# Moving a skip term from diagonal matmuls to GpSimd, with tanh gates and early parameters, in a scan-and-gate kernel

## The chip, the cores and the metric

The kernel runs on one core of one Trainium2 chip. The metric is the device time of one execution in microseconds (us); most numbers are medians of several runs. The kernel before takes 203.13 us (median of 3 runs, 202.52 to 203.82).

Engines are named as in the profile: PE is TensorE (PEld its weight loads), DVE is VectorE, ACT is ScalarE, POOL is GpSimd, SP is the engine that issues most DMA. A name with q after it (ACTq) is that engine's sequencer.

## The reference

The input has 2048 tokens of width D = 448; types are bf16. After a layer norm two branches read the same `xn`: a state-space scan over time, and a gated feed-forward block of width F = 1792.

```python
def _A_ref(x, ...):                     # scan branch, complex state of 448
    Bu = einsum("bld,pd->blp", x, B_bar)
    for t in range(L):
        h = Lam_bar * h + Bu[:, t, :]
    return 2.0 * einsum("blp,dp->bld", hseq, Cmat).real + x * Dskip   # the skip term

def _B_ref(x, w_gate, w_up, w_down):    # feed-forward branch
    h = sigmoid(x @ w_gate) * (x @ w_up)
    return h @ w_down

x = A_x
xn = layernorm(x)
s = _A_ref(xn, ...)
g = silu(_B_ref(xn, w_gate, w_up, w_down))
return x + s * g
```

## The kernel before

The 2048 tokens go through in four chunks of 512, each of four tiles of 128. Every operation is handed to a small planner with an engine, an estimated cost and its dependences; the planner then fixes the order on each engine. So a change of one part can reorder all. TensorE makes, for each chunk, 14 gate and up groups ("gu" buffers in PSUM, three of them), the scan's input groups (also in "gu"), four down groups and four output groups y (two "acc" buffers). VectorE does the scan and its rotations.

The parts that the change touches:

```python
# gate and up evacuation, chunks 1 to 3: ScalarE empties both halves of PSUM
add("ACT", ..., lambda: A.activation(sig[b][:], gu[a][:], ACT.Sigmoid), ...)
...
add("ACT", ..., lambda: A.copy(out=ub[b][:], in_=gu[a][:]), r=[("gu", a)], w=[("ub", b)])
add("DVE", ..., lambda: V.tensor_tensor(out=ho, in0=sig[sb_][:], in1=ub[b][:], op=ALU.mult), ...)

# chunk 0 already uses tanh, and VectorE reads the up half from PSUM:
#   ho = (tanh(gate / 2) + 1) * up

# down output: silu as sigmoid times copy
add("ACT", ..., lambda: A.activation(sigd[b][:], d, ACT.Sigmoid, scale=half), ...)
add("ACT", ..., lambda: A.activation(zb[b][:], d, ACT.Copy, scale=half), ...)
add("DVE", ..., lambda: V.tensor_tensor(out=g_t[g][:], in0=zb[b][:], in1=sigd[b][:], op=ALU.mult), ...)

# output group y: the skip term xn * Dskip as four matmuls with a diagonal matrix
for i, (hm, cm) in enumerate(K_ORDER):
    T.matmul(y, lhsT=hT[c % 2][:, hm, js], rhs=cT[:, cm, c0:c1], start=(i == 0), stop=(i == 6))
    if i:
        continue
    for k in range(4):
        ...
        T.matmul(y[:, a0 - c0:a1 - c0], lhsT=xnT[c % 3][:, 2 * k, js], rhs=diag[:, a0:a1], ...)
...
add("DVE", ..., lambda: V.tensor_tensor(out=od, in0=y, in1=g_t[g][:, c0:c1], op=ALU.mult), ...)
add("DVE", ..., lambda: V.tensor_tensor(out=od, in0=od, in1=x_all[:, t, c0:c1], op=ALU.add), ...)
```

The scan's parameters (three vectors, and Dskip) are loaded last on GpSimd's queue, and the cos/sin tables are made from them in the middle of chunk 0.

## Time and profile before

| | before |
|---|---|
| time, median of 3 | 203.13 us |
| span of the profiled run | 199.6 us |
| TensorE, VectorE, ScalarE, GpSimd busy | 184.7, 157.7, 115.5, 42.8 us |
| TensorE clock | 1.00 in all windows but the last (the clock records begin at 13.72 us) |

From the page of the kernel before: the busy time of each engine, with its share of the span and number of instructions, then rows of busy tenths in 40 equal slices of the span, of 5.0 us here.

```profile
PE 184.7 (93%) x1479; PEld 91.9 (46%) x1486; DVE 157.7 (79%) x298; ACT 115.5 (58%) x160; POOL 42.8 (21%) x94
PE   7498999994999999997998999999999999999991
DVE  4700599998999999999999999997897999340163
POOL 6400387258261181062061000000000000000000
```

TensorE is the fullest engine. VectorE shows a row of nines, with one eight, from about 25 to 135 us. GpSimd has nothing at all to do after about 110 us.

The table of ten-microsecond windows of the kernel before. The columns are the window and its length, then busy us (and instructions) of PE, PEld, DVE, ACT and POOL, then the granted TensorE clock, the DMA share and GB/s.

```profile
10.00:20.00 10.00, 9.12 (x196) 7.68 (x194) 0.00 (x0) 5.72 (x6) 0.23 (x1) 1.00 1.17 244
...
40.00:50.00 10.00, 7.02 (x62) 3.04 (x58) 9.25 (x16) 9.88 (x17) 6.86 (x16) 1.00 0.96 243
...
100.00:110.00 10.00, 9.16 (x70) 4.61 (x71) 9.79 (x21) 6.87 (x9) 4.04 (x7) 1.00 0.23 60
...
150.00:160.00 10.00, 9.97 (x74) 5.07 (x75) 8.71 (x14) 7.06 (x11) 0.00 (x0) 1.00 0.01 2
```

Between 10 and 20 us VectorE does nothing. Between 40 and 50 us TensorE loses 3 us while ScalarE is full. In the 100 to 110 window VectorE is at 98% and TensorE at 92%. The 1.00 of the first window hides a slow start: the timeline shows TensorE's matmuls of the first gate groups 0.106 us apart until 13.73 us and 0.055 after that, and the clock records only begin at 13.72.

Groups of instructions of the kernel before (line, engine, operation, output and inputs, count, then busy us, mean ns of one, and idle time before them with its cause).

```profile
L727 DVE TENSOR_TENSOR_SCAN wv<-c_r,st,z 128x512 bf16<-128x512 f32 x18 | 22.9, 1279 | 0.2
L639 DVE TENSOR_TENSOR hF<-sig,ub 128x1024 bf16<-128x1024 bf16 x21 | 14.3, 686 | 4.0 <-ACT ub L638 3.9
L741 DVE TENSOR_TENSOR ta<-wv,cosT 128x1024 bf16<-128x1024 bf16 x12 | 8.1, 678 | 0.1
L822 PE MATMUL acc<-diag,xnT 128*128 128x128 bf16 (+1 forms) x60 | 5.4, 212 | 0.0
```

The timeline of VectorE in the same kernel (start, duration) shows what one instruction costs when others follow at once: they overlap a little, so the step from start to start is the better measure, 0.60 us for `ta`, 1.19 us for the scan.

```profile
95.23 0.69 DVE L741 TENSOR_TENSOR ta<-wv,cosT 128x1024 bf16<-128x1024 bf16 x1
...
97.67 1.28 DVE L727 TENSOR_TENSOR_SCAN wv<-c_r,st,z 128x512 bf16<-128x512 f32 x1
```

What TensorE waited for (total us, times, longest) was most of all ScalarE, emptying PSUM:

```profile
PE gu L660 <- ACT sig L628: 3.4, 2, 2.3
```

And the head on ScalarE in the kernel before (the first square root of the layer norm starts at 4.79 us):

```profile
3.05 1.28 ACT L328 ACT_TABLE_LOAD   x1 [3.05 <-issue]
...
4.79 0.30 ACT L356 ACTIVATE sdb<-veb 128x1 bf16<-128x1 bf16 x2 [0.45 <-DVE mv L347]
```

### The profile page before, as it was taken

Reading aid. Unit: us, or ns where it says so; the run is one execution under the profiler, and the core shown is the slowest. Engines: PE = TensorE matmul, PEld = TensorE weight load, DVE = VectorE, ACT = ScalarE, POOL = GpSimd, SP = SyncE. Lnnn points to the kernel's source line nnn. Section 1 sums busy time; section 2 is a strip of 40 time slices with the busy share of each in tenths; the row PEclk is TensorE's granted clock in tenths of the full one; section 3 lists DMA queues with packets and bytes.
Section 4 is the critical chain, followed back from the end, with each engine's and each line's share of the span. In section 5 each row is a group of like instructions: output and inputs, shape, how many; then the busy total and the mean of one; then the engine's idle time right before and its main releaser. Section 6 shows DMA issues by size and latency. Waiting matters only on the chain.

```text
span 199.6 us, 3751 instructions
## 1 busy us (share of the span) xinstructions
PE 184.7 (93%) x1479; PEld 91.9 (46%) x1486; DVE 157.7 (79%) x298; ACT 115.5 (58%) x160; POOL 42.8 (21%) x94
## 2 busy tenths in 40 slices
PE   7498999994999999997998999999999999999991
PEld 2386444441445444443544444444545444455561
DVE  4700599998999999999999999997897999340163
ACT  2319691799799978527839461846547653411320
POOL 6400387258261181062061000000000000000000
PEclk9999999999999999999999999999999999999998
DMA  5999606489700014302103200000000000010011
GB/s 158 241 322 164 134 8 89 93 245 240 211 0 0 3 26 90 68 3 54 38 25 88 53 23 3 0 23 26 0 23 0 3 23 0 26 49 23 0 42 52
DMA packets 29218, 13.32 MB, mean 67 GB/s; under 512 B 19728, under 2 KB 29200, under 8 KB 29200
## 3 DMA queue, kind: packets, MB, share of 16 engines
q1 hardware_dynamic: 26928, 11.25, 24.3%
q10 hardware_dynamic: 2144, 1.84, 3.6%
q8 instruction: 11, 0.18, 0.4%
q14 instruction: 7, 0.06, 0.1%
q0 software_dynamic: 128, 0.00, 0.1%
HBM read 6.66 MB, written 1.84 MB: 43 GB/s over the span
## 4 chain that ended last, share of the span: by engine, by line
PE 58%; DVE 20%; ACT 11%; DMA 4%; POOL 3%; issue 3%; SPq 0%; ACTq 0%; POOLq 0%
PE gu L609 25%; PE acc L788 9%; PE acc L816 8%; PE gu L788 5%; PE gu L673 4%; DVE wv L727 4%; DMA wG<-in_B_w_gate_dram 4%; DVE hF L639 2%; DVE bst L346 2%; ACT bus L684 1%; ACT ub L638 1%; DVE wv L759 1%; DVE z L723 1%; PE acc L822 1%; POOL rsd L363 1%
## 5 line engine op out<-in xcount | busy, mean ns | idle before, releaser
L609 PE MATMUL gu<-xnT,wG 64*128 64x512 bf16 (+1 forms) x259 | 48.2, 335 | 2.8 <-DMA wG<-in_B_w_gate_dram 2.0
L610 PE MATMUL gu<-xnT,wG 64*128 64x512 bf16 (+1 forms) x259 | 48.2, 334 | 0.0
L609 PE MATMUL gu<-xnT,wU 64*128 64x512 bf16 x196 | 46.0, 376 | 0.0
L610 PE MATMUL gu<-xnT,wU 64*128 64x512 bf16 x196 | 46.0, 376 | 0.0
L788 PE MATMUL acc<-wd,hF 128*128 128x448 bf16 x168 | 33.8, 353 | 0.0
L609 PEld LDWEIGHTS <-wG 64*128 64x128 bf16 x259 | 21.9, 100 | 23.4 <-issue 2.4
L788 PEld LDWEIGHTS <-hF 128*128 128x128 bf16 x224 | 21.5, 98 | 21.3 <-issue 2.1
L609 PEld LDWEIGHTS <-wU 64*128 64x128 bf16 x196 | 18.0, 94 | 23.9 <-issue 2.1
L628 ACT ACTIVATE sig<-gu 128x1024 bf16<-128x1024 f32 x21 | 21.5, 1023 | 12.2 <-PE gu L610 12.2
L638 ACT CAST ub<-gu 128x1024 bf16<-128x1024 f32 x21 | 21.2, 1010 | 8.2 <-PE gu L610 8.2
L816 PE MATMUL acc<-cT,hT 128*128 128x448 bf16 x105 | 24.4, 353 | 0.0
L727 DVE TENSOR_TENSOR_SCAN wv<-c_r,st,z 128x512 bf16<-128x512 f32 x18 | 22.9, 1279 | 0.2
L610 PEld LDWEIGHTS <-wG 64*128 64x128 bf16 x259 | 21.9, 99 | 1.0 <-issue 1.0
L610 PEld LDWEIGHTS <-wU 64*128 64x128 bf16 x196 | 18.0, 94 | 0.0
L639 DVE TENSOR_TENSOR hF<-sig,ub 128x1024 bf16<-128x1024 bf16 x21 | 14.3, 686 | 4.0 <-ACT ub L638 3.9
L684 ACT CAST bus<-gu 128x1024 bf16<-128x1024 f32 x12 | 12.1, 1009 | 8.8 <-PE gu L673 8.8
L673 PE MATMUL gu<-xnT,bT 128*128 128x512 bf16 x65 | 15.3, 379 | 1.1 <-issue 1.1
L798 DVE TENSOR_TENSOR g_t<-zb,sigd 128x448 bf16<-128x448 bf16 x16 | 6.1, 388 | 12.8 <-ACT zb L797 12.8
L816 PEld LDWEIGHTS <-hT 128*128 128x128 bf16 x119 | 10.4, 98 | 7.3 <-issue 0.4
L796 ACT ACTIVATE sigd<-acc 128x448 bf16<-128x448 f32 x12 | 6.5, 540 | 12.5 <-PE acc L788 12.5
L377 ACT ACTIVATE xn<-x_all,nmr,rsd 128x448 bf16<-128x448 bf16 x12 | 8.9, 758 | 4.1 <-POOL nmr L365 4.1
L346 DVE BATCH_NORM_STATS2 bst<-x_all 128x6 f32<-128x448 bf16 x16 | 9.4, 611 | 2.0 <-DMA x_all<-in_A_x_dram 2.0
(138 smaller groups left out, 276.3 us busy)
## 6 DMA issues: line engine op xcount, KB each, us to landing
out_dram<-o_t SPq DMA_DIRECT2D x15, 112.0 KB, 1.7
wd<-in_B_w_down_dram SPq DMA_DIRECT2D x1, 1568.0 KB, 7.3
x_all<-in_A_x_dram SPq DMA_DIRECT2D x3, 448.0 KB, 4.8
wG<-in_B_w_gate_dram ACTq DMA_DIRECT2D x1, 448.0 KB, 7.9
wG<-in_B_w_gate_dram SPq DMA_DIRECT2D x1, 448.0 KB, 9.9
wU<-in_B_w_up_dram ACTq DMA_DIRECT2D x1, 448.0 KB, 12.3
wU<-in_B_w_up_dram SPq DMA_DIRECT2D x1, 448.0 KB, 13.2
xnT<-xn SPq DMA_TRANSPOSE x24, 2.4
```

The costliest lines, as they stand in the source:

```text
L346: add("DVE", 0.53, lambda: V.bn_stats(out=bst[b][:], in_=x_all[:, t, :]), r=[("x", t)], w=[("bst", b)])
L377: add("ACT", 0.65, lambda: A.activation(xn[b][:, 0:448], x_all[:, t, :], ACT.Identity, bias=nmr[:, t, :], scale=rsd[:, t, :]), r=[("x", t) ...
L609: T.matmul(gu[a][:, 0, ts], lhsT=w_[0:H, s, ms], rhs=x[0:H, s, ts], start=(s == 0), stop=(s == 6))
L610: T.matmul(gu[a][:, 1, ts], lhsT=w_[H:P, (s + 1) % 7, ms], rhs=x[H:P, s, ts], start=(s == 0), stop=(s == 6))
L628: add("ACT", act(1024), lambda: A.activation(sig[b][:], gu[a][:], ACT.Sigmoid), r=[("gu", a), "sinL", "cosL", "sth", "cth"] + [(s, p) for ...
L638: add("ACT", act(1024), lambda: A.copy(out=ub[b][:], in_=gu[a][:]), r=[("gu", a)], w=[("ub", b)])
L639: add("DVE", dve2(1024), lambda: V.tensor_tensor(out=ho, in0=sig[sb_][:], in1=ub[b][:], op=ALU.mult), r=[("sig", sb_), ("ub", b)], w=hk)
L673: T.matmul(gu[a][:, i, :], lhsT=bT[:, kt, i, pt * P:pt * P + P], rhs=x[:, 2 * kt, :], start=False, stop=(kt == 2))
L684: add("ACT", act(1024), lambda u=u, a=a: A.copy(out=bus[u][:], in_=gu[a][:]), r=[("gu", a)], w=[("bus", u)])
L727: dve(1.194, lambda k=k: V.tensor_tensor_scan(out=wv[:, k, :], data0=rb, data1=z[:, k, :], initial=(st[pt][:, k, :] if c else 0.0), op0=AL ...
L788: T.matmul(d, lhsT=hF[c % 2][:, m, h, js], rhs=wd[:, ft, :], start=(ft == 0), stop=(ft == FT - 1))
L816: T.matmul(y, lhsT=hT[c % 2][:, hm, js], rhs=cT[:, cm, c0:c1], start=(i == 0), stop=(i == 6))
```

## The change

Its intent: take 16 groups of diagonal matmuls from TensorE and give the skip term to GpSimd, which is idle for half the span; take the up copies from ScalarE; and bring the parameters in early, so that the tables are made while VectorE has nothing else to do. A new backward pass of the planner comes with it, which respects that an engine does one thing at a time. The core of the diff:

```diff
-# planner: late times by the longest path behind each operation
+# planner: late times by a backward pass that fills each engine (about 35 lines)
...
-    for k, vec in enumerate((A_log_dt, A_Lambda_im, A_Lambda_re, A_Dskip)):
-        load("POOL", ("vrow", k), ...)                    # after all weights
+    load_w("SP", "g", 0, 0)                               # first, smaller weight block
+    load_w("ACT", "g", 1, 0)
+    for k, vec in enumerate((A_log_dt, A_Lambda_im, A_Lambda_re)):
+        load("ACT" if k < 2 else "SP", ("vrow", k), ...)  # before the other blocks
...
-                add("ACT", ..., lambda: A.copy(out=ub[b][:], in_=gu[a][:]), ...)
-                add("DVE", ..., lambda: V.tensor_tensor(out=ho, in0=sig[sb_][:], in1=ub[b][:], op=ALU.mult), ...)
+            add("DVE", ..., lambda: V.scalar_tensor_tensor(out=ho, in0=th, scalar=1.0, in1=gu[a][:],
+                                                           op0=ALU.add, op1=ALU.mult), ...)   # all chunks
...
-        sigmoid, copy and multiply of the down output
+        add("ACT", ..., lambda: A.activation(g_t[g][:], d, ACT.Silu, scale=0.5), ...)
...
+        add("POOL", 0.7, lambda: G.tensor_scalar(out=xq, in0=x_all[:, t, :], scalar1=rsd[:, t, :], scalar2=nmr[:, t, :], ...))
+        add("POOL", 1.3, lambda: G.tensor_tensor(out=xq, in0=xq, in1=dbc[:], op=ALU.mult), ...)
...
-                    for k in range(4):
-                        T.matmul(y[...], lhsT=xnT[...], rhs=diag[:, a0:a1], ...)
-            add("DVE", ..., V.tensor_tensor(out=od, in0=y, in1=g_t, op=ALU.mult))
-            add("DVE", ..., V.tensor_tensor(out=od, in0=od, in1=x_all, op=ALU.add))
+            add("DVE", ..., V.tensor_tensor(out=od, in0=y, in1=xq, op=ALU.add))
+            add("DVE", ..., V.tensor_tensor(out=od, in0=od, in1=g_t, op=ALU.mult))
+            if late:   # the last seven tiles
+                add("DVE", ..., V.tensor_tensor(out=od, in0=od, in1=x_all, op=ALU.add))
+            else:      # the first nine
+                add("POOL", 1.3, ..., G.tensor_tensor(out=od, in0=od, in1=x_all, op=ALU.add))
```

GpSimd so gets 41 operations on 128x448 elements: 16 scale-and-shift, 16 multiplies, 9 adds.

## The prediction

> **What bounds it now.** The page gives TensorE 184.7 us of a 199.6 us span, VectorE 157.7, ScalarE 115.5, GpSimd 42.8. In the table of ten-microsecond windows TensorE is full except for: the head (first real matmul at 9.7 us, released by the gate weights' DMA; the timeline shows its first matmuls 0.106 us apart, later ones half that), 40-50 us (7.0 busy), 90-110 us (17.9 of 20) and the end. In 40-50 ScalarE is 9.9 busy: the timeline has cos/sin activations, an activation table load of 1.28 us and gate evictions in one row. From 57 to 104 us the chain of waits runs through VectorE (97-99% busy, 50-130 us), then through TensorE to the end. VectorE is idle in 10-20 us and for about 20 us after 170.
>
> **What the change removes.**
> - TensorE: 16 groups of diagonal matmuls, 0.19 us of pitch each in the timeline: -3.1 us, on the critical path.
> - ScalarE: 21 up-copies (1.01 us), half of the 32 activations of 0.54 us, one of four table loads: about -31 us, mostly not critical itself.
> - Stalls: parameters and tables move into the idle 10-20 us of VectorE (about 7 us of table work), so cos/sin leave the crowded 36-46 us. Of the 3 us stall there about 2.5 go; of the 2.1 us at 90-110 perhaps 1.
> - Head: smaller first weight blocks and extra warm-up matmuls: -1.5 to -2.5 us.
> Sum: about -9 us.
>
> **What it adds.**
> - VectorE: 21 gate products of tanh and PSUM at the 1.13 us pitch that chunk 0 already shows, instead of 0.60: +11. Gate products of the down output go (16 x 0.30): -5. Late adds (8 x 0.30): +2.5. Net +9.
> - GpSimd: 16 x (scale-and-shift + multiply) and 8-9 adds of 128x448. No such op is in this trace[...].
> - Contention: [...]
>
> VectorE so gets about 157.7 + 9 + 15 = 182 us; its room is the 10-20 us gap and the slack after 170, since chunk 3's scan can slip to about 185. It becomes co-critical with TensorE, and the planner does not know of the contention: I give back 2 to 3 us, since PSUM of the up half is now freed by VectorE. Net -6.5.
>
> **Prediction.** 196.5 us, 8 in 10 within 190.5 to 203. Faster by over 2%: 0.67; within: 0.30; slower: 0.03.
>
> **What would show it.** TensorE busy falls to about 180 and the 40-50 us stall is gone; the first eviction in the head comes 1.5-2.5 us earlier; ScalarE falls to about 85; VectorE rises to 175-185, with tensor-tensor means above the present 684 ns; GpSimd rises to 70-85; new TensorE waits name the VectorE gate product.
>
> **What would make it wrong.** Slower: GpSimd holds VectorE longer than estimated, so gate products free PSUM late and TensorE stalls through 60-160 us; or the skip term comes late and blocks the two accumulator banks; or up weights, now all issued by one queue, come late. Faster: contention hides wholly in VectorE slack; then 190 to 193.

Two terms are cut from it, since they rested on what no trace of this case shows: how long GpSimd's large operations take (behind the 70 to 85 us of GpSimd busy time), and how they hold VectorE. The second was the author's estimate, and enters as the 15 us in VectorE's 182 and in the 2 to 3 us given back. The sum, with these terms, came to -9 us from what the change removes, and with 2 to 3 given back to a net -6.5, from 203.1 us to about 196.5.

## The result, and the profile after

The kernel after is correct and slower: 213.51 us (median of 4 runs, 211.67 to 215.47, one of them slow) against 202.82 (202.16 to 203.82) of the kernel before on the same chip. The ratio is 1.049, with a 95% interval of 1.040 to 1.058. All ratios here are the mean time of one kernel's fast runs over the mean of the other's of the same rounds, so they are not quite the ratio of the medians beside them. The profiled run took 213.84 us, with a span of 212.1.

| | before | after |
|---|---|---|
| time, median | 202.82 us | 213.51 us |
| TensorE busy | 184.7 | 187.3 |
| VectorE busy | 157.7 | 178.9 |
| ScalarE busy | 115.5 | 87.0 |
| GpSimd busy | 42.8 | 92.7 |
| first gate eviction starts | 17.37 | 19.34 |
| first down group starts | 52.0 | 51.9 |
| fourth, ninth, tenth down group | 81.0, 140.6, 151.8 | 85.4, 147.2, 164.7 |

The last three rows are start times in us, read from the timelines. They say where the time was lost: not in the first 52 us, where a late head is made good by the cured stall of the 40 to 50 us window, but after it: 4.5 us by the fourth down group, 6.7 by the ninth, and another 6.3 in one step between the ninth and the tenth, which start 17.5 us apart instead of 11.2.

The page after:

```profile
PE 187.3 (88%) x1419; PEld 90.5 (43%) x1426; DVE 178.9 (84%) x286; ACT 87.0 (41%) x122; POOL 92.7 (44%) x126
PE   7398899999989969999959899998946999999990
DVE  3579358699999999999999999999999599965064
POOL 3138728000996755013997712354252080557000
```

TensorE's row (slices of 5.3 us here) has new holes: a 6, a 5, and a 4 followed by a 6. VectorE's nines now run without a break from about 42 to 164 us.

The same windows after, and one more:

```profile
10.00:20.00 10.00, 9.51 (x189) 7.92 (x189) 8.90 (x29) 6.40 (x9) 5.08 (x13) 0.69 1.26 225
...
40.00:50.00 10.00, 9.61 (x79) 4.33 (x76) 9.90 (x14) 6.45 (x9) 0.00 (x0) 1.00 1.01 262
...
100.00:110.00 10.00, 7.61 (x59) 3.37 (x58) 10.00 (x18) 5.09 (x7) 9.59 (x12) 1.00 0.26 49
...
150.00:160.00 10.00, 6.15 (x51) 2.64 (x50) 9.83 (x14) 2.59 (x3) 4.91 (x4) 0.97 0.03 11
160.00:170.00 10.00, 9.07 (x38) 4.32 (x40) 7.47 (x10) 4.00 (x7) 0.39 (x1) 0.69 0.03 11
```

VectorE's gap at 10 to 20 us is filled (0.00 busy became 8.90) and the stall between 40 and 50 us is gone (7.02 became 9.61), both as intended. In 100 to 110 and 150 to 160 us VectorE is full, GpSimd works beside it, and TensorE falls to 7.61 and 6.15. In the window after that TensorE looks busy, with 38 matmuls only, at a mean clock of 0.69. A wait of 4.45 us ends at 160.60 us, and the clock records show half the clock from 159.47 to 166.30; in the 3.41 us before 159.47 TensorE was busy for 0.09 us. The same records show half the clock from 77.55 to 80.96 too, a stretch of 3.41 us; in the 3.41 us before it TensorE was busy for 1.58 us and its longest wait was 1.45. But after the 3.41 us from 108.27, with TensorE busy for 1.50, the clock stayed full. What decides between the two these records don't show.

TensorE's loss after 52 us can so be added up. Its waits of over 0.15 us sum to 12.8 us there, against 2.6 in the kernel before. In the two stretches at half the clock it was busy for 8.8 us, so that about 4.4 us went to the clock (an estimate: half of these, since matmuls of 64x512 follow each other 0.43 us apart from 77.55 to 80.96 us, and 0.22 after that). Less the 3.1 us of diagonal matmuls that it no longer has (the prediction's figure, from a pitch of 0.19 us for each of 16 groups), this makes 11.5 us, against 12.5 between the spans of the two profiled runs.

Groups after:

```profile
L746 DVE TENSOR_TENSOR_SCAN wv<-c_r,st,z 128x512 bf16<-128x512 f32 x18 | 25.7, 1431 | 0.0
L657 DVE SCALAR_TENSOR_TENSOR hF<-sig,gu 128x1024 bf16<-128x1024 f32 x21 | 25.2, 1205 | 0.0
L760 DVE TENSOR_TENSOR ta<-wv,cosT 128x1024 bf16<-128x1024 bf16 x12 | 10.0, 836 | 0.1
L830 POOL TENSOR_SCALAR xd<-x_all,rsd,nmr 128x448 bf16<-128x448 bf16 x12 | 16.5, 1374 | 48.3 <-DVE o_t L850 47.5
L837 POOL TENSOR_TENSOR xd<-xd,dbc 128x448 bf16<-128x448 bf16 x16 | 19.4, 1211 | 16.0 <-DMA dbc<-in_A_Dskip_dram 15.1
L858 POOL TENSOR_TENSOR o_t<-o_t,x_all 128x448 bf16<-128x448 bf16 x9 | 13.1, 1452 | 6.6 <-DVE o_t L852 5.6
```

The scan and `ta` are the same instructions as before, and their means rose from 1279 to 1431 ns and from 678 to 836. What stretches them is seen when VectorE's and GpSimd's timelines are laid beside each other. VectorE:

```profile
106.81 2.05 DVE L746 TENSOR_TENSOR_SCAN wv<-c_r,st,z 128x512 bf16<-128x512 f32 x1
108.78 1.19 DVE L657 SCALAR_TENSOR_TENSOR hF<-sig,gu 128x1024 bf16<-128x1024 f32 x1
...
111.53 1.53 DVE L760 TENSOR_TENSOR ta<-wv,cosT 128x1024 bf16<-128x1024 bf16 x1
```

GpSimd in the same time:

```profile
106.33 1.45 POOL L858 TENSOR_TENSOR o_t<-o_t,x_all 128x448 bf16<-128x448 bf16 x1
107.74 1.63 POOL L400 TENSOR_TENSOR sdb<-veb,halfc 128x2 bf16<-128x2 bf16 x1
...
111.48 1.03 POOL L837 TENSOR_TENSOR xd<-xd,dbc 128x448 bf16<-128x448 bf16 x1
```

The scan at 106.81 takes 2.05 us; a GpSimd add is in progress. `ta` at 111.53 takes 1.53 us instead of 0.68; a GpSimd multiply had begun 0.05 us earlier. The gate product at 108.78, which has one input in PSUM, runs at its usual 1.19. Over the whole trace, the step of a scan is 1.57 us in the mean beside a large GpSimd operation and 1.20 without one, and that of the gate product 1.130 and 1.125. A delay is seen the other way too: the GpSimd operation on two elements at 107.74, a power, took 1.63 us, and the same instruction takes 0.71 at 23.25 us of this trace, where VectorE is idle.

In this document the *stretch* of a trace is the sum, over VectorE instructions that follow each other without idle time, of the step from start to start, less the median step of the same group where no GpSimd operation ran beside it. Groups that have no such clear sample are left out. It is 0.4 us before and 11.3 us after. It depends on how instructions are grouped: a recount from the same traces with other groupings gave 12 to 13 us for after, and moved the figures below by up to 2 us. Read them with that margin.

What TensorE waits for, after:

```profile
PE gu L682 <- DVE hF L657: 6.9, 2, 4.5
PE acc L437 <- DVE xn L408: 3.2, 1, 3.2
PE gu L679 <- DVE hF L657: 2.0, 3, 1.1
PE gu L640 <- DVE hF L657: 1.7, 2, 1.3
```

Three of the four name the gate product on VectorE, which now frees the PSUM buffers. The second is in the head. There ScalarE shows this:

```profile
3.62 1.28 ACT L366 ACT_TABLE_LOAD   x1 [3.62 <-DMA x_all<-in_A_x_dram]
3.78 3.45 ACTq L328 DMA_DIRECT2D wG<-in_B_w_gate_dram  x2
7.33 0.48 ACT L394 ACTIVATE sdb<-mv,epsc 128x1 bf16<-128x1 bf16 x2 [2.43 <-DMA wG<-in_B_w_gate_dram]
```

The issue of two weight blocks holds ScalarE's sequencer for 3.45 us, and the first square root starts at 7.33 us instead of 4.79. TensorE waits 3.2 us for the normalised tile, until 8.39 us, and the clock records show half the clock from 9.28 to 16.11.

### The profile page after: what moved, and what is told of

Read it like the earlier page. It is cut to its first block, busy times and chain, and to the rows that moved or that the text cites. A ratio compares the mean times of both kernels' runs of the same rounds, so it can differ in the third digit from the quotient of the medians.

```text
span 212.1 us, 3642 instructions
## 1 busy us (share of the span) xinstructions
PE 187.3 (88%) x1419; PEld 90.5 (43%) x1426; DVE 178.9 (84%) x286; ACT 87.0 (41%) x122; POOL 92.7 (44%) x126
## 4 chain that ended last, share of the span: by engine, by line
DVE 48%; PE 38%; issue 6%; DMA 2%; ACT 2%; POOL 1%; ACTq 1%; DVEq 0%
PE gu L640 17%; DVE wv L746 9%; DVE hF L657 8%; PE acc L807 7%; PE acc L844 5%; PE gu L807 5%; DVE ta L739 3%; DVE tb L740 3%; DVE z L742 3%; DVE o_t L850 3%; DVE hT L763 2%; DVE cT L609 2%; DMA wG<-in_B_w_gate_dram 2%; DVE bst L385 2%; DVE tb L761 2%
## 5 line engine op out<-in xcount | busy, mean ns | idle before, releaser
L640 PE MATMUL gu<-xnT,wG 64*128 64x512 bf16 (+1 forms) x259 | 50.0, 344 | 3.5 <-DVE hF L657 1.7
L641 PE MATMUL gu<-xnT,wG 64*128 64x512 bf16 (+1 forms) x259 | 50.1, 344 | 0.0
L830 POOL TENSOR_SCALAR xd<-x_all,rsd,nmr 128x448 bf16<-128x448 bf16 x12 | 16.5, 1374 | 48.3 <-DVE o_t L850 47.5
L654 ACT ACTIVATE sig<-gu 128x1024 f32<-128x1024 f32 x21 | 21.4, 1021 | 37.9 <-PE gu L641 35.6
L837 POOL TENSOR_TENSOR xd<-xd,dbc 128x448 bf16<-128x448 bf16 x16 | 19.4, 1211 | 16.0 <-DMA dbc<-in_A_Dskip_dram 15.1
L746 DVE TENSOR_TENSOR_SCAN wv<-c_r,st,z 128x512 bf16<-128x512 f32 x18 | 25.7, 1431 | 0.0
L657 DVE SCALAR_TENSOR_TENSOR hF<-sig,gu 128x1024 bf16<-128x1024 f32 x21 | 25.2, 1205 | 0.0
L844 PE MATMUL acc<-cT,hT 128*128 128x448 bf16 x105 | 22.0, 353 | 1.4 <-DVE hT L763 1.4
L850 DVE TENSOR_TENSOR o_t<-acc,xd 128x448 bf16<-128x448 f32 x15 | 9.2, 613 | 11.6 <-PE acc L844 11.6
L858 POOL TENSOR_TENSOR o_t<-o_t,x_all 128x448 bf16<-128x448 bf16 x9 | 13.1, 1452 | 6.6 <-DVE o_t L852 5.6
L813 ACT ACTIVATE g_t<-acc 128x448 bf16<-128x448 f32 x12 | 6.5, 538 | 14.8 <-PE acc L807 14.8
```

The lines of the kernel that those rows point to most:

```text
L640: T.matmul(gu[a][:, 0, ts], lhsT=w_[0:H, s, ms], rhs=x[0:H, s, ts], start=(s == 0), stop=(s == 6))
L641: T.matmul(gu[a][:, 1, ts], lhsT=w_[H:P, (s + 1) % 7, ms], rhs=x[H:P, s, ts], start=(s == 0), stop=(s == 6))
L654: add("ACT", act(1024), lambda: A.activation(th, gu[a][:], ACT.Tanh, scale=0.5), r=[("gu", a)], w=[tk])
L657: add("DVE", dve1(1024), lambda: V.scalar_tensor_tensor(out=ho, in0=th, scalar=1.0, in1=gu[a][:], op0=ALU.add, op1=ALU.mult), r=[("gu", a) ...
L746: dve(1.194, lambda k=k: V.tensor_tensor_scan(out=wv[:, k, :], data0=rb, data1=z[:, k, :], initial=(st[pt][:, k, :] if c else 0.0), op0=AL ...
L830: add("POOL", 0.7, lambda: G.tensor_scalar(out=xq, in0=x_all[:, t, :], scalar1=rsd[:, t, :], scalar2=nmr[:, t, :], op0=ALU.mult, op1=ALU.add),
```

## The experiments

Five theories were on the table.

- A: large GpSimd operations that read SBUF hold up VectorE instructions that take two inputs from SBUF, and VectorE, now full, sets TensorE's pace (a hypothesis; the trace shows the scan's step at 1.57 us beside them and 1.20 without).
- B: the tanh gates are to blame: VectorE instead of ScalarE frees the up half of PSUM, with a 1.13 us instruction instead of a 0.60 us one.
- C: the skip term comes late from GpSimd and blocks the accumulators; contention is beside the point.
- D: the head: the early parameter loads stand before the weights on ScalarE's queue and hold ScalarE.
- E: the new planner's order is worse.

A differs from C in one prediction: under A it matters whether GpSimd *reads* SBUF. That it matters was an assumption when the runs were planned, and so was that an input in PSUM spares a VectorE instruction: e3 tests the first, and on the second there are the steps of the gate product, 1.130 us beside large GpSimd operations and 1.125 without.

Edits are against the kernel after unless another is named. "Wrong" means that the output is not the reference's (relative error 0.605 in all three such runs) because the skip term is empty; these kernels measure time only.

Two things help in reading the runs. In e1 and e3, VectorE and ScalarE have the instructions of the kernel after in the same order, and in e12 those of e2, as their traces show; e8 and e13 share one order with each other, but it is not that of after, and in e2, e4, e7 and e11 the planner has reordered the work too. And where an expectation names a range and the time falls outside it, this is said.

### e1_skip_emptied: no skip work on GpSimd (wrong)

```diff
-            add("POOL", 0.7, lambda: G.tensor_scalar(out=xq, ...), ...)
+            add("POOL", 0.7, lambda n=xd_n[0]: G.memset(xq, 0.0) if n <= NXD else None, ...)
-        add("POOL", 1.3, lambda: G.tensor_tensor(out=xq, in0=xq, in1=dbc[:], op=ALU.mult), ...)
+        add("POOL", 1.3, lambda: None, ...)
```

The planner still counts the same costs, so the order on TensorE, VectorE and ScalarE is the same as after; only GpSimd's work is gone, but for the nine adds.

> Changed kernel, same order on TensorE, VectorE, ScalarE and the DMA queue; the 32 GpSimd operations that make the skip term are emptied (each of the four buffers is zeroed once; wrong result on purpose). Theory A (large GpSimd operations that read SBUF hold VectorE; in the trace VectorE steps beside them are about 13 us longer in sum, some 9 us of it beside these 32): 202 to 206 us, VectorE scans back at 1.28 us mean. Rival B (VectorE's tanh-times-PSUM product is 0.53 us longer than before, 21 times, and that alone makes VectorE the limit): stays at 210 to 214.

Measured: 205.64 us (202.38 to 207.06; the kernel before 202.56 beside it). Two of its four runs count as slow. VectorE's busy time fell from 178.9 to 166.4 us with the same 286 instructions, the stretch from 11.3 to 2.4. The scan is nearly back:

```profile
L746 DVE TENSOR_TENSOR_SCAN wv<-c_r,st,z 128x512 bf16<-128x512 f32 x18 | 23.7, 1320 | 0.0
```

So GpSimd's skip work costs about 8 us by the medians, or 9 by the means of the fast runs alone (203.8 here, 212.9 for the kernel after). They were run at other times. Whether by contention or by lateness this run does not say, since both are gone.

### e3_skip_writes_only: GpSimd as late, but writing only (wrong)

```diff
-            add("POOL", 0.7, lambda: G.tensor_scalar(out=xq, ...), ...)
+            add("POOL", 0.7, lambda: (G.memset(xq, 0.0), G.memset(xq, 0.0)), ...)
-        add("POOL", 1.3, lambda: G.tensor_tensor(out=xq, in0=xq, in1=dbc[:], op=ALU.mult), ...)
+        add("POOL", 1.3, lambda: (G.memset(xq, 0.0), G.memset(xq, 0.0)), ...)
```

> Changed kernel, same order everywhere; each of the 32 skip operations is replaced by two memsets of the same tile (wrong result on purpose), so GpSimd is still busy about 1 us per operation and VectorE still waits for the tile, but GpSimd reads no SBUF. Theory A[...]: as e1 within 2 us. Rival C (the skip term or the norm statistics come late because GpSimd is busy[...]): stays within 2 us of the changed kernel, 211 to 214.

Measured: 207.17 us (205.86 to 209.7), ratio 1.029 (1.018 to 1.040). GpSimd is 79.4 us busy, but VectorE's scan is as in e1:

```profile
L746 DVE TENSOR_TENSOR_SCAN wv<-c_r,st,z 128x512 bf16<-128x512 f32 x18 | 23.7, 1323 | 0.0
L837 POOL MEMSET xd<- 128x448 bf16 x32 | 15.1, 471 | 1.6
```

Two writes of 0.47 us in the place of each operation leave VectorE nearly alone: the stretch is 2.9, against 11.3 with the operations that read SBUF and 2.4 with neither (e1). And GpSimd being busy and in the same order, the time is near e1's: theory C is hard to hold, with two reservations: the pair of writes is somewhat shorter than the operations it replaces, and by the fast runs alone (206.7 against 203.8 in e1) 2.9 us are left, a little more than the 2 that were allowed. e12 settles it.

### e8_last_add_on_vector: the nine adds back on VectorE

```diff
-            if late:
+            if True:
```

> Changed kernel with the add of x on VectorE for all sixteen tiles, in place of nine adds on GpSimd. Theory A: nine GpSimd operations fewer free some 3 us of VectorE, nine adds at 0.30 us take 2.7 of it back: 211 to 214, no clear difference.

Measured: 206.38 us (205.45 to 207.48), ratio 1.021 (1.014 to 1.027). I had expected 211 to 214 and no clear difference; it gained 7 us by the medians, 6 by the ratios. Nine more instructions on the engine that is full make the kernel *faster*: each add on VectorE is a step of 0.30 us, each on GpSimd ran 1.45 us, and the stretch fell to 5.8 us. As the adds moved to VectorE, the planner also put other VectorE work in another order, and this run doesn't show how much of the gain that makes.

### e13_no_large_gpsimd: both, so no large GpSimd operation (wrong)

```diff
 # e1, and
-            if late:
+            if True:
```

> Changed kernel with the 32 skip operations emptied (wrong result on purpose) and the nine adds of x on VectorE: no large GpSimd operation is left, VectorE does even 2.7 us more. If the two parts of the GpSimd work simply add up (8 us and 7 us by single removal), 198 to 200 us; if either alone already brings VectorE back within its slack, 203 to 206, little below the single removals (205.64 and 206.38).

Measured: 201.86 us (200.97 to 203.02), ratio 1.004 (0.996 to 1.012), between the two ranges expected. The stretch is 0 and the scan is at its old cost:

```profile
L746 DVE TENSOR_TENSOR_SCAN wv<-c_r,st,z 128x512 bf16<-128x512 f32 x18 | 22.9, 1275 | 0.1
```

Against after that is 11.6 us by the medians and 9 us by the ratios (1.049 less 1.004, of 202 us), for a stretch of 11 to 13 us. So most of the time that GpSimd held VectorE became time of the kernel. Against e8, which has the same order on VectorE, the 32 operations alone are worth 4.5 us by the medians and 3.4 by the ratios. e1 and e8 gained 8 and 7, more than the whole in sum; perhaps either of them already frees part of VectorE's tightest stretch and they share it, which I did not test. VectorE is 165.8 us busy here, nine adds included; by that the contention was nearer to 16 us (178.9 less 165.8, and about 3 for the adds), part of it in places where VectorE had slack.

This run shows a second thing. Contention is gone, TensorE has no diagonal matmuls, and still the kernel is no faster than the one before. None of the 9 us that the prediction took off for the rest of the change is seen here. Part of that is the late head: the first down group starts at 54.1 us, against 52.0 before. And VectorE makes nine adds more here than in the change (2.7 us).

### e2_diag_back: the diagonal matmuls back, all else as after

```diff
-        add("POOL", 0.7, ... G.tensor_scalar(out=xq, ...))
-        add("POOL", 1.3, ... G.tensor_tensor(out=xq, in0=xq, in1=dbc[:], op=ALU.mult))
+                    for k in range(4):
+                        T.matmul(y[...], lhsT=xnT[c % 3][:, 2 * k, js], rhs=diag[:, a0:a1], ...)
-            y + xq, * g_t on VectorE, + x_all on VectorE or GpSimd
+            y * g_t, + x_all on VectorE
+    load("POOL", ("vrow", 3), D * 2, vrow[3:4, :], A_Dskip.unsqueeze(0), cost=0.8)   # a fourth early parameter
```

> Changed kernel with the skip term back in diagonal matmuls and the last add back on VectorE; tanh gates, early parameters and the new planner stay. Theory A: TensorE has 3 us more work but nothing holds VectorE: 198 to 204 us. Rival B: 208 or more.

Measured: 204.05 us (202.2 to 204.9), ratio 1.014 (1.004 to 1.025), correct, stretch 0.4, at the upper edge of the 198 to 204 that theory A gave. So the loss of the change goes with the skip term. But without it the rest, tanh gates and early parameters, is no gain either.

### e7_skip_alone_on_before: the skip term alone, on the kernel before

```diff
 # against the kernel before: its yout replaced by the one of after, diag removed
```

> The kernel before with only the skip term moved to GpSimd and VectorE (old gates, old head, old planner). Theory A: VectorE is held 10 us or more beside its bf16 products, so 208 to 214 us although TensorE has 3 us less to do. If the loss needs the tanh gates too: 200 to 204.

Measured: 219.20 us (218.4 to 220.66), ratio 1.085 (1.077 to 1.092), above both ranges expected, with a stretch of 20.1 us. The old gate product takes both inputs from SBUF, and here it takes 866 ns in the mean instead of 686.

```profile
L635 DVE TENSOR_TENSOR hF<-sig,ub 128x1024 bf16<-128x1024 bf16 x21 | 18.1, 866 | 4.9 <-ACT sig L624 3.1 <-ACT ub L634 1.7
```

The four corners are now measured: neither part 202.3 (its medians), the skip term alone 219.2, the rest alone 204.05, both 213.5. So the rest of the change *softens* the damage by some 7 us. That need not be the tanh gates' doing alone: the rest includes the new planner, which is worth about 7 us by itself in e11. With their product, which reads one input from PSUM, the stretch is smaller (11.3 us in the kernel after, with the old product 20.1 here and 18.4 in e4).

### e4_old_gates: the old gates in the kernel after

```diff
 # gu_evac and the silu of the down output as in the kernel before
```

> Changed kernel with the gates of before in chunks 1 to 3 (sigmoid and copy on ScalarE, bf16 product on VectorE at 0.60 us) and the down gate as sigmoid, copy and product; skip term by GpSimd stays. Rival B: 202 or less. Theory A alone: little change or slower, 208 to 214[...]. If both count, about 206.

Measured: 215.27 us (213.74 to 216.07), ratio 1.071 (1.060 to 1.081): slower than after by 2 us of the medians or 4 of the ratios, 1 us above theory A's range, stretch 18.4. Theory B falls: undoing the tanh gates makes it worse. The gate product takes 827 ns in the mean here, near the 866 of e7, against 686 in the kernel before.

### e12_diag_and_spare_gpsimd: GpSimd work that nobody waits for

Against e2, after the last add of each output tile:

```diff
+            G.tensor_tensor(out=scr[0][:, 0:n], in0=od, in1=x_all[:, t, c0:c1], op=ALU.add)
+            G.tensor_scalar(out=scr[1][:, 0:n], in0=x_all[:, t, c0:c1], scalar1=rsd[:, t, :], scalar2=None, op0=ALU.mult)
+            if not late:
+                G.tensor_tensor(out=scr[2][:, 0:n], in0=x_all[:, t, c0:c1], in1=x_all[:, t, c0:c1], op=ALU.mult)
```

The results are never read. The output stays correct.

> The kernel with diagonal matmuls back (204.05 us) plus GpSimd work that nobody waits for: after each output tile two or three operations of 128x448 that read SBUF and write spare tiles, in number and size like those of the change. VectorE, TensorE and ScalarE have the same instructions in the same order. Theory A[...]: 210 to 215, VectorE's tensor-tensor pitches stretched by 8 us or more in sum. Rival C (only waiting for the skip term costs): 203 to 206.

Measured: 215.98 us (215.6 to 216.35), 1 us above theory A's range, ratio 1.075 (1.064 to 1.085), against 1.014 of e2: about 12 us for work without a single consumer. Stretch 11.5. The scan rises from e2's mean to after's, and the wait for the gate product grows, from 0.3 us in e2. First e2's scan:

```profile
L751 DVE TENSOR_TENSOR_SCAN wv<-c_r,st,z 128x512 bf16<-128x512 f32 x18 | 22.9, 1278 | 0.0
```

Then e12's scan:

```profile
L752 DVE TENSOR_TENSOR_SCAN wv<-c_r,st,z 128x512 bf16<-128x512 f32 x18 | 25.7, 1434 | 0.0
```

And the first of TensorE's waits in e12:

```profile
PE gu L685 <- DVE hF L663: 4.5, 2, 4.2
```

This is the strongest support of A: no result of this work is used, VectorE and ScalarE have the same instructions in the same order as in e2, and the lost time is about the stretch. There are two other ways in which it could act, and the trace lets one look at both. The first spare operation reads an output tile, so that the next writer may have to wait for it: this shows once, for 0.4 us. And GpSimd's own small operations for the layer norm come later: but after 52 us every wait of TensorE above 0.2 us, 8.1 us in all, names the gate product of VectorE. In this trace too the clock is halved twice after waits (of 4.2 and 2.6 us), from 142.64 and from 159.71 us for 3.41 us each (the granted clock is 0.83 from 140 to 150 us and 0.84 from 160 to 170), so that not all of the 12 us is waiting.

### e11_old_planner: the old backward pass

```diff
-        (the new backward pass)
+        for o in reversed(self.ops):
+            for b, kind in o.suc:
+                x = b.late - self._gap(o, b, kind) - o.cost
+                ...
+                o.late = min(o.late, x)
```

> Changed kernel with the backward pass of the planner of before. Rival E (the new order of work makes the loss): 207 or less. Theory A: the order matters little, 211 to 217.

Measured: 220.65 us (220.22 to 221.65), ratio 1.098 (1.089 to 1.107), outside both ranges, stretch 16.3. The order does matter, but the other way: the new planner is worth about 7 us in this kernel; theory E falls. I did not take apart how.

### e5_vectors_off_act_queue and e6_diag_and_head: all parameters on GpSimd's queue

```diff
-        load("ACT" if k < 2 else "SP", ("vrow", k), ..., cost=0.25)
+        load("POOL", ("vrow", k), ..., cost=0.8)
```

e5 is this edit alone, e6 is e2 with it.

> Changed kernel with one difference: the three parameter vectors are loaded from the GpSimd queue, as before, so that the ScalarE queue has five loads instead of seven. Theory D (in the head the seventh load on the ScalarE queue waits for the first weight block to land at 6.6 us[...], so the first square root moves from 4.8 to 7.3 us and TensorE idles 3.2 us[...]): first square root back near 4.8 us, first gate matmul at 9.5 us or earlier, and 209 to 212 us in all, as VectorE, the limit afterwards, also starts earlier. If the head's delay is swallowed by later slack: 212 to 214.

> The kernel with diagonal matmuls back (204.05 us) plus the vectors off the ScalarE queue. Theory D: it follows TensorE, so the head is worth 2 to 4 us here: 200 to 202 us, a little under before. If the head is not what eats its gain: 203 to 205.

Measured: e5 217.04 us (216.86 to 217.16), ratio 1.073 (1.067 to 1.079); e6 203.34 (202.47 to 204.53), ratio 1.006 (0.999 to 1.012). e5 missed both its ranges; e6 fell into the range of its alternative, but for another reason. In e6 the first square root does start early, at 3.96 us, but from GpSimd's queue the vectors land late, and TensorE waits before the small matmuls that turn them to columns. In e6:

```profile
PE acc L477 <- DMA hF<-in_A_Dskip_dram: 3.9, 1, 3.9
```

One wait was traded for another, so these two say nothing on D.

### e9_one_vector_per_queue: one vector on each of three queues

```diff
-        load("ACT" if k < 2 else "SP", ("vrow", k), ..., cost=0.25)
+        load(("POOL", "ACT", "SP")[k], ("vrow", k), ..., cost=0.25)
```

> Changed kernel with one parameter vector on each of the three queues (GpSimd, ScalarE, SyncE), so that ScalarE has six loads before its first square root and the vectors still land early. Theory D (the seventh load blocks ScalarE): first square root near 4.8 us, no wait of TensorE for the parameter columns (in the run with all three on the GpSimd queue they came late), first down group near 49 us instead of 51.9; in all 209 to 213, for afterwards VectorE sets the pace.

Measured: 212.64 us (211.9 to 213.47), ratio 1.057 (1.048 to 1.067). With one load less in front, ScalarE's issue of the two weight blocks takes 1.29 us and the square root starts at 4.70:

```profile
3.29 1.29 ACTq L328 DMA_DIRECT2D wG<-in_B_w_gate_dram  x2
4.70 0.50 ACT L394 ACTIVATE sdb<-mv,epsc 128x1 bf16<-128x1 bf16 x2 [0.27 <-DVE bst L385]
```

So D is right on the head: the first down group starts at 49.8 us instead of 51.9. But it is worth nothing that can be told from noise in the whole: the scatter of the rounds is larger than the 0.9 us between the medians, and the stretch is 14.1. Two microseconds that are there at 50 us are not there at the end, after VectorE's full part.

The raw records of the kernel after name the cause. The last of the three gate-weight issues on ScalarE waits until 6.61 us on the completion semaphore that the first weight block, issued at 1.67 us, still uses; the program gives it the same one. It is a wait that the program contains, from how completion semaphores are handed out. Whether anything else in the chip limits the number of loads on a queue, these runs don't show.

### e10_diag_one_vector_per_queue, e15_best_again: what the experiments point to

Against e2: the load line of e9, and Dskip in a row of its own, turned to columns later.

```diff
-    load("POOL", ("vrow", 3), D * 2, vrow[3:4, :], A_Dskip.unsqueeze(0), cost=0.8)
+    load("POOL", "drow", D * 2, drow[:, :], A_Dskip.unsqueeze(0), cost=0.8)
...
+        if i == 8:
+            dcols()        # in chunk 0's gate and up steps: four matmuls, two copies, then diag
```

> Diagonal matmuls back, one vector per queue, and the skip vector in a row of its own, turned into columns only in chunk 0. Theory D: head 3 to 4 us shorter than in the kernel with diagonal matmuls at 204.05: 199 to 202 us, at or below before. If the tanh gates and early parameters cost something in the steady part: 203 or more with an early head.

> The kernel of 198.10 us again, five rounds, for an interval: 197 to 200 us, 1 to 2 per cent under before.

Measured: e10 198.10 us (197.28 to 199.32), ratio 0.986 (0.976 to 0.995); e15, the same kernel again on another chip with more rounds, 199.06 (197.91 to 199.64), ratio 0.989 (0.983 to 0.995). It is correct, and 1.1 to 1.5% under the kernel before: a real gain by the intervals, but within the 2% that count as the same. 

Here the better head does count: of the 2.9 us between the profiled runs of e2 and e10 (202.2 and 199.32), 2.7 are there at the first down group (53.5 and 50.8).

### e14_best_with_old_gates: what the tanh gates are worth without contention

```diff
 # e10 with gu_evac and the silu of the down output as in the kernel before
```

> The kernel of 198.10 us (diagonal matmuls, one vector per queue, skip row apart) with the gates of before. If the tanh gates pay without GpSimd contention: 200 to 203. If ScalarE has room for the old gates once the tables are early: 197 to 199, no difference.

Measured: 201.53 us (199.42 to 201.87), ratio 0.999 (0.989 to 1.009), beside e15's 0.989. The tanh gates may so be worth about 1%, but the intervals overlap and this is not shown.

## Why the prediction was wrong

The prediction was 196.5 us with a range to 203, and the kernel takes 213.5. Point by point:

- *TensorE's 16 diagonal groups, about 3 us.* Right in kind: at the end of the kernel, where output groups follow each other, their step fell from 1.5–1.7 us to 1.3. But TensorE's busy time rose from 184.7 to 187.3 instead of falling to 180: the clock records have 17.1 us at half the clock, in which TensorE was busy for 15.3, and matmuls take longer there (the tenth down group 3.58 us, the ninth 2.81). In e13, with 3.4 us of it, TensorE was busy for 183.1.
- *ScalarE about 31 us less.* Right: 28.5.
- *The stall at 40 to 50 us goes.* Right: 7.02 us busy became 9.61.
- *VectorE at 175 to 185, GpSimd at 70 to 85.* VectorE was 178.9, right; GpSimd 92.7, a little over. My GpSimd durations came from no trace. From 187 to 196 us, where VectorE is busy for 4.9 of 9 us, the multiply took 1.04 to 1.05 us; over all 16, most of them beside a full VectorE, 1.21 in the mean. The scale-and-shift took 0.71 to 0.91 us at its least disturbed, 1.37 in the mean of the 12 of chunks 1 to 3 and 3.13 at most; the form of chunk 0 took 2.27 in the mean of four.
- *Contention on VectorE, 15 us in the sum (the estimate).* Right in size: 11 to 13 us of stretch, about 16 by busy times.
- *New TensorE waits name the VectorE gate product.* Right: 6.9, 2.0 and 1.7 us.
- *The head 1.5 to 2.5 us earlier.* Wrong in sign: the first eviction came 2 us later, because one load too many on ScalarE's queue reused a semaphore still in use and held ScalarE for 3.45 us (e9 undoes that).
- *Of all contention "I give back 2 to 3 us".* **This is the step that failed.** I took VectorE's room to be the gap at 10 to 20 us and the slack after 170, and set the contention against that sum. The gap was taken by the table work that the change itself moves there, the slack after 170 comes after the damage, and in between, from 50 to 130 us, VectorE was already 97 to 99% busy before the change. In that stretch there was next to no room for longer instructions, and TensorE now waits for VectorE to free its buffers. Taking the large GpSimd operations away brought 9 to 12 us (e13), and adding useless ones to a kernel without them cost 12 (e12).
- *The sum "about -9 us".* **This failed too**, and makes up about as much of the miss of 17 us: with contention and diagonal matmuls both gone, e13 is at 1.004 of the kernel before, not 9 us below it. The head's sign is part of it. With the head mended and the diagonal matmuls back, the rest of the change (tanh gates, early parameters, planner) gained 1.1 to 1.5%, 2 to 3 us (e15, e10), where the prediction's head and stalls alone made 5 to 6. In e10 the first eviction comes 2.1 us earlier than before, but the first down group only 1.2. Which of the terms fell short besides the head was not taken apart.

The misses of the head and of the contention do not simply add. With the contention left in, mending the head was worth 0.9 us by the medians, within the scatter (e9). With it gone, the head counts, and the kernel with diagonals and a mended head (e10, e15) lands at 198 to 199. That this lies inside the range that I had given is chance: the range was for the kernel with the skip term moved.

My list of what would make the prediction wrong had the cause in its first entry ("GpSimd holds VectorE longer than estimated, so gate products free PSUM late"), but with the wrong condition: it held VectorE about as long as estimated; what was off was how little of it VectorE could absorb, and, outside that list, how little the rest of the change gained.

What stays open: how the old planner loses 7 us in e11, why the terms of the -9 us other than the head gained so little, and what a kernel with the skip term moved and a mended head would take without contention (no such run exists), and what a kernel with the skip term moved but Dskip's product made by another engine would take.

## What to carry to other kernels

An engine's slack has to be counted where the new load falls, window by window: here work on "idle" GpSimd that reads SBUF was paid by VectorE's instructions with two SBUF inputs in that same window (the scan's step 1.57 us beside it, 1.20 without), and as VectorE set the pace there, nearly one to one (e12: 12 us for a stretch of 11.5). Before moving work there, ask for each VectorE instruction of the window whether both its inputs come from SBUF; here the gate product, with an operand in PSUM, took as long beside large GpSimd operations as otherwise (1.130 and 1.125 us). To price such a move, a copy of the planned GpSimd work without any consumer (as e12) is a quick test that leaves the output right. And when a change bundles several parts, run the rest without the disputed part (as e2 and e13): here that would have shown that the rest alone brought nothing.
